# A limit of three loads under way, new orders under that limit, and the first keys issued first, in a fused attention and expert kernel

## The chip, the cores and the metric

The kernel runs on one core of one Trainium2 chip. The metric is device time in microseconds (us): the median of several runs, and beside it one execution taken by the hardware profiler. The engines are named as in the profile: PE is TensorE's matrix multiplication and PEld its weight loads, DVE is VectorE, ACT is ScalarE, POOL is GpSimd, SP is SyncE, which issues most DMA transfers.

## What is computed

Attention over 8 samples, 12 heads, 448 positions and head size 64, all in float32, with scores capped by a tanh; then, per sample, the 128 positions with the highest gate scores go through a two-layer expert.

```python
scores = q @ k^T / sqrt(64)
scores = cap * tanh(scores / cap)                     # cap is 30
attn   = exp(scores - max) / (sum + 1e-9)
x      = (attn @ v), heads side by side               # 8 x 448 x 768
s      = x @ w_gate
top    = the 128 rows of a sample with the largest s
out[top] = x[top] + sigmoid(s[top]) * (relu(x[top] @ w1) @ w2)   # w1 768x1024, w2 1024x768
out[others] = x[others]
```

## The kernel before

The work is cut into 24 "doubles": three groups of four heads for each of the 8 samples. A double needs three loads (`Double.load`, line 620 issues them): queries, keys and values, each of about 450 KB, into rings of two buffers with a third that is lent at the start (`qlent`, `klent`, `vlent`). Its keys are taken in four chunks, three of 128 and one of 64; the two 64-chunks of neighbouring doubles share one unit. For each unit TensorE writes scores into PSUM (`scores_mm`, lines 681 and 691), ScalarE takes the tanh (lines 1252 and 1298) and then the exponential (lines 1261 and 1305) into a buffer `p`, and TensorE multiplies by the values (`values_mm`, line 706), summing over the four chunks in the one PSUM accumulator `psV`. Before the next double may start its values, `evac` (lines 737 to 743) empties that accumulator on VectorE in two halves. From the fifth double on, queries and keys are split into a high and a low part (lines 647 and 653, VectorE), and the scores are three matmuls instead of one.

Six PSUM banks (`psE`) serve the scores at first, so that the scores of one unit are written while ScalarE reads those of another; two of them are needed later for the expert's matmuls. After `SIX` units (20) the six are closed, four become the one score buffer `psS`, and two become `psT`, in which everything of the expert stage is computed.

The weights come in 14 tiles (`weights_proc`, line 555): six of 512 KB and eight of 384 KB, over three staging buffers (`stage` twice, `hs`). VectorE splits each into two parts (lines 567 and 570). The gate weights (`load_gate`, line 541) are one load of 576 KB. When a sample's three doubles are scored (line 772), `select_proc` finds the 128 rows: the scores go to memory and come back as a row (lines 810 and 813), VectorE ranks them (lines 842 and 850) and writes a one-hot matrix (line 881), TensorE picks the row numbers (line 891), and GpSimd gathers the rows (line 909). `expert_proc` transposes them (line 938), multiplies by w1 and w2 in `group` (line 992), and scatters the result (line 1058); the last sample goes through `halves` (lines 1086 and 1104).

The order of all instructions is set when the program is built. `Sim` is a planner: each `Task` has an engine, an estimated duration, what it depends on and which buffers it takes; each engine takes the task that can start first, with ties settled by priorities, which the table `EARLIER` shifts task by task. For TensorE the string `SCRIPT` says which kind comes next: `Q` is the scores of a unit (or half of one), `V` the values of one, and a number behind a letter is how many expert matmuls may come in before. The numbers of the planner put no instruction into the program; they only set its order. On the chip the engines run their instructions in this order and wait for each other by semaphores.

TensorE's instructions have three shapes here: quarter (64 rows by 64 columns: the unsplit scores and the 64-key chunks of the values), tall (128 by 64: the other values) and wide (everything else: split scores and the expert).

The program starts with `first_loads` (lines 1573 to 1578): queries, the cap, the first keys and the rest of the first double, before a branch on the cap's size (line 1714). `warm_up` multiplies zeros on TensorE from line 1588 on until the first keys are there.

Of the kernel before, what the change touches and what calls it, by code (L numbers as in the profile page):

```python
# [8 lines left out]
F32 = mybir.dt.float32  # L9
# [7 lines left out]
P = 128  # L17
# [12 lines left out]
HOLD = 1000  # L30

# [4 lines left out]
SCRIPT = ("Q Q Q1 V Q3 Q V Q4 Q24 V Q1 V2 Q6 Q9 V6 Q1 Q V12 Q Q38 Q V6 Q12 V Q Q15 Q V5 Q3 Q12 "  # L36
# [6 lines left out]

EARLIER = {('evac', 0): -0.4, ('evac', 1): 0.4, ('evac', 3): 0.4, ('evac', 4): -3, ('evac', 5): -1,
           ('evac', 6): 3, ('evac', 7): -3, ('evac', 9): -1, ('evac', 10): 3, ('evac', 11): -3,
           ('evac', 12): 0.4, ('evac', 13): -0.4, ('evac', 17): 1, ('evac', 20): 3, ('evac', 22):
           -1, ('evac', 23): 0.4, ('evac', 25): 3, ('evac', 26): -1, ('evac', 27): 0.4, ('evac',
           28): 0.4, ('evac', 29): 1, ('evac', 30): 1, ('evac', 31): 1, ('evac', 33): 1, ('evac',
           34): -0.4, ('evac', 35): 0.4, ('evac', 36): 1, ('evac', 37): -3, ('evac', 38): 0.4,
           ('evac', 39): 0.4, ('gate', 0): -0.4, ('gate', 1): -3, ('gate', 3): 1, ('gate', 4):  # L50
           -0.4, ('gate', 5): 1, ('gate', 6): 1, ('gate', 7): -0.4, ('gate', 8): 3, ('gate', 11):
           1, ('gate', 12): -1, ('gate', 13): 0.4, ('gate', 14): 3, ('gate', 15): -0.4, ('gate',
# [146 lines left out]

QUARTER, TALL, WIDTH = range(3)  # L200
SWITCH = 40
AFTER = {(TALL, WIDTH): 104, (TALL, QUARTER): 102, (QUARTER, WIDTH): 90, (QUARTER, TALL): 70,
         (WIDTH, TALL): 100, (WIDTH, QUARTER): 60}
MARGIN = 150
RESERVE = 50000
# [1577 lines left out]
```

## Time and profile before

| | us |
|---|---|
| median of 3 runs | 437.09 (436.97 to 438.45) |
| the profiled execution, its own time | 437.59 |
| its span, first to last instruction | 435.8 |
| PE busy in the span | 420.6 |
| ACT busy in the span | 305.7 |
| DVE busy in the span | 278.9 |

The span is what the profiler's trace covers; 1.8 us of the execution's own time lie around it. A busy time is the sum over an engine's instructions, counted once where they overlap. An idle time in a row of the trace stands in square brackets behind the instruction that ended it, with what released it. "issue" there means that nothing the profile shows was waited for. Matmuls are pipelined and their ends are modelled, so a PE busy time holds small pauses too.

### The profile page before, as it was taken

The numbers are of one execution on the slowest core, as the hardware profiler recorded it, in microseconds if no ns is written. First come the engines' busy times: TensorE is split into PE (matmuls) and PEld (weight loads), VectorE is DVE, ScalarE is ACT, GpSimd is POOL, SyncE is SP. The second block draws the span as 40 slices with busy tenths as digits, with TensorE's granted clock in tenths as the row PEclk, the third lists the DMA queues.
The fourth block names the chain that finished last, engine by engine and source line by source line (L and its number), as shares of the span: only waits on it lengthen the run. The fifth ranks groups of instructions, "written<-read, shape, count | busy, mean of one in ns | idle before, by whom it ended". The sixth has DMA issues, their size and how long they took to land.

```text
span 435.8 us, 17858 instructions
## 1 busy us (share of the span) xinstructions
PE 420.6 (96%) x8080; PEld 354.6 (81%) x8080; DVE 278.9 (64%) x862; ACT 305.7 (70%) x197; POOL 26.9 (6%) x73
## 2 busy tenths in 40 slices
PE   8989998999999999999999999999999999999994
PEld 5646677788789888899889978989788898879894
DVE  1586978859852788559754885837937685267241
ACT  5999999697895588695697676969787698411000
POOL 1100010100010000010000100101000010000101
PEclk9999999899999999999999999999999999999998
DMA  7996558370460481373170470463361421230202
GB/s 232 396 388 199 169 161 262 106 240 27 120 259 3 137 267 31 107 245 108 44 282 15 144 245 17 122 214 106 90 236 43 127 86 47 74 69 2 74 3 77
DMA packets 33268, 60.73 MB, mean 139 GB/s; under 512 B 10304, under 2 KB 20288, under 8 KB 33184
## 3 DMA queue, kind: packets, MB, share of 16 engines
q1 hardware_dynamic: 31600, 52.73, 37.4%
q0 software_dynamic: 1440, 6.56, 4.8%
q8 instruction: 65, 1.06, 1.0%
q10 hardware_dynamic: 144, 0.23, 0.1%
q14 instruction: 19, 0.16, 0.1%
HBM read 45.33 MB, written 14.17 MB: 137 GB/s over the span
## 4 chain that ended last, share of the span: by engine, by line
PE 82%; DMA 6%; ACT 5%; DVE 3%; issue 2%; SPq 0%; POOL 0%; POOLq 0%; DVEq 0%; ACTq 0%
PE psV L706 29%; PE psT L992 23%; PE psS L681 16%; PE psB L992 4%; PE psS L691 3%; DMA vlent<-in_v 2%; DMA stage<-in_moe_w 2%; PE psE L681 2%; PE psE L691 2%; ACT p L1252 2%; ACT p L1261 1%; PE psT L938 1%; PE psV L992 1%; DMA p<-out,idx 1%; ACT plent L1261 1%
## 5 line engine op out<-in xcount | busy, mean ns | idle before, releaser
L706 PEld LDWEIGHTS psV<-v,p 128*64 128x64 f32 (+1 forms) x3864 | 104.8, 137 | 21.7 <-issue 15.1
L706 PE MATMUL psV<-v,p 128*64 128x65 f32 (+1 forms) x3864 | 111.6, 223 | 4.5 <-issue 2.4
L1298 ACT ACTIVATE p<-psS,sc 128x1792 f32<-128x1792 f32 x48 | 84.1, 1753 | 39.1 <-PE psS L681 23.2
L1305 ACT ACTIVATE p<-p,capc 128x1792 f32<-128x1792 f32 x48 | 86.1, 1794 | 1.4
L681 PE MATMUL psS<-qh,kh 64*128 64x448 f32 x220 | 43.1, 388 | 0.0
L706 PEld LDWEIGHTS psV<-v,plent 128*64 128x64 f32 (+1 forms) x1288 | 34.7, 137 | 7.9 <-issue 3.0
L737 DVE RECIPROCAL rec<-psV 128x7 f32<-128x7 f32 x48 | 9.5, 199 | 48.5 <-PE psV L706 48.5
L1298 ACT ACTIVATE plent<-psS,sc 128x1792 f32<-128x1792 f32 x16 | 28.0, 1753 | 17.7 <-PE psS L681 8.9
L706 PE MATMUL psV<-v,plent 128*64 128x65 f32 (+1 forms) x1288 | 37.4, 222 | 1.9 <-POOL vlent L667 1.2
L772 DVE CUSTOM_DVE_ANT_0 jk<-xn,gates 128x256 bf16<-128x256 f32 x72 | 30.3, 421 | 1.5
L1305 ACT ACTIVATE plent<-plent,capc 128x1792 f32<-128x1792 f32 x16 | 28.7, 1793 | 0.5
L738 DVE TENSOR_TENSOR xn<-psV,rec 128x384 f32<-128x384 f32 x48 | 26.8, 557 | 1.7
L1261 ACT ACTIVATE p<-p,capc 128x1792 f32<-128x1792 f32 x14 | 25.1, 1792 | 0.5
L1252 ACT ACTIVATE p<-psE,sc 128x1792 f32<-128x1792 f32 x14 | 24.3, 1738 | 0.9 <-PE psE L681 0.5
L842 DVE TENSOR_SCALAR_CACHE_REDUCE jk<-row,score 128x512 bf16<-128x512 f32 (+1 forms) x32 | 23.7, 742 | 0.9
L681 PEld LDWEIGHTS psS<-qh,kh 64*128 64x128 f32 x220 | 20.9, 187 | 2.6 <-ACT p L1298 0.2
L647 DVE CAST kh<-k 128x896 fp32r<-128x896 f32 x20 | 12.5, 626 | 14.0 <-PE psS L681 10.6
L681 PE MATMUL psS<-qlent,kh 64*128 64x448 f32 x112 | 20.9, 370 | 0.0
L681 PE MATMUL psS<-qh,klent 64*128 64x448 f32 x112 | 20.9, 370 | 0.0
L992 PE MATMUL psT<-w2h,hh 64*128 64x384 f32 x192 | 20.3, 340 | 0.6 <-POOL fence L975 0.6
L992 PE MATMUL psT<-w2l,hh 64*128 64x384 f32 x192 | 20.7, 336 | 0.0
L691 PE MATMUL psE<-q,k 64*64 64x448 f32 x176 | 19.7, 548 | 0.4 <-ACT p L1252 0.4
(180 smaller groups left out, 686.4 us busy)
## 6 DMA issues: line engine op xcount, KB each, us to landing
v<-in_v SPq DMA_DIRECT2D x23, 455.0 KB, 4.4
q<-in_q SPq DMA_DIRECT2D x22, 448.0 KB, 5.5
k<-in_k SPq DMA_DIRECT2D x22, 448.0 KB, 6.0
out<-xn SPq DMA_DIRECT2D x24, 384.0 KB, 4.7
stage<-in_moe_w SPq DMA_DIRECT2D x4, 512.0 KB, 8.5
stage<-in_moe_w SPq DMA_DIRECT2D x5, 384.0 KB, 4.4
row<-line SPq DMA_DIRECT2D x7, 256.0 KB, 3.6
out<-xt SPq DMA_DIRECT2D x48, 32.0 KB, 4.0
```

The lines of the kernel that those rows point to most:

```text
L647: nc.vector.tensor_copy(t.slots[0].obj, self.at(nm))
L681: done += [tc.nc.tensor.matmul(banks[2 * r + j][:, :K.S], lhsT=a[HALF[j], r, c * P:(c + 1) * P], rhs=b[HALF[j], r, :], start=(n == 0), sto ...
L691: done += [tc.nc.tensor.matmul(banks[n][HALF[half], :K.S], lhsT=k[HALF[j], r, at:at + HD], rhs=q[HALF[j], r, :], start=True, stop=True).ins]
L706: tc.nc.tensor.matmul(D.acc.obj[HALF[g], r, i * WIDE:(i + 1) * WIDE], lhsT=p[rows, h, n * HD:(n + 1) * HD], rhs=v[rows, u, :], start=(c == ...
L738: nc.vector.tensor_tensor(slots[0].obj.rearrange("p c (r j d) -> p r j c d", r=2, j=2)[:, r], blocks[:, :2 * full, :K.D].rearrange("p (j c ...
L772: nc.vector.tensor_tensor_reduce(out=K.jk[:, :x.shape[1]], in0=x, in1=g, scale=1.0, scalar=0.0, op0=ALU.mult, op1=ALU.add, accum_out=part[ ...
L842: nc.vector.tensor_scalar(K.jk[:m], row[:m], score[:m, c:c + 1], None, op0=ALU.is_gt, op1=ALU.add, accum_out=rk.obj[:m, 0, c:c + 1])
L992: ins = nc.tensor.matmul(bank.obj[:, g, :width], lhsT=pair.obj[part][HALF[h], i, :], rhs=K.wts[r][HALF[h], i, g * width:(g + 1) * width], ...
L1252: a = nc.scalar.activation(slot.obj, K.S6[:, 2 * lo:2 * lo + 4, :K.S], AF.Tanh, scale=K.sc)
L1261: nc.scalar.activation(slot.obj, slot.obj, AF.Exp, scale=K.cap)
L1298: nc.scalar.activation(slot.obj, K.S4[:, :, :K.S], AF.Tanh, scale=K.sc)
L1305: nc.scalar.activation(slot.obj, slot.obj, AF.Exp, scale=K.cap)
```

## The change

Four things are done.

1. At most three loads are under way. `in_flight` keeps the loads of the doubles, of the weights and of the gate weights in one list, and each from the fourth on waits on SP, by a semaphore, for the landing of the one three places before. The planner knows this limit too (`Sim.ready`). Stores and the row DMAs are not counted.
2. The planner has other costs: one price per shape that TensorE changes into (`AFTER`), durations of matmul groups, and a price for the fetching of TensorE's own instructions in blocks of 256 (`stall`). `SIX` is 19 instead of 20. `SCRIPT` and `EARLIER` are new. A scatter also waits in the plan for the one before it (`SWEEP`).
3. The first keys are the first DMA on SP; the cap goes to ACT's queue, behind the first queries.
4. `warm_up` multiplies a constant tile of zeros instead of one that VectorE first clears.

```diff
 HOLD = 1000
+SWEEP = 400
+CHUNK, FIRST_EDGE, BEGUN, FETCH, SHARE, DEEP = 256, 193, 71, 2350, 0.5, 8000
+LOADS = 3
+LOAD = ("load", "wload", "wg")
...
-SCRIPT = ("Q Q Q1 V Q3 Q V Q4 Q24 V Q1 V2 Q6 Q9 V6 Q1 Q V12 Q Q38 Q V6 Q12 V Q Q15 Q V5 Q3 Q12 "
+SCRIPT = ("Q3 Q Q12 V29 Q20 Q18 V26 Q2 Q V16 Q2 V4 Q16 Q8 Q14 V1 Q6 V Q6 Q14 V Q20 Q V2 Q2 Q Q "
...
-EARLIER = {('evac', 0): -0.4, ('evac', 1): 0.4, ('evac', 3): 0.4, ('evac', 4): -3, ('evac', 5): -1,
+EARLIER = {('evac', 0): -0.4, ('evac', 1): 1, ('evac', 5): 3, ('evac', 6): 0.4, ('evac', 7): -0.4,
...
-AFTER = {(TALL, WIDTH): 104, (TALL, QUARTER): 102, (QUARTER, WIDTH): 90, (QUARTER, TALL): 70,
-         (WIDTH, TALL): 100, (WIDTH, QUARTER): 60}
+AFTER = (141, 141, 195)
...
-SIX = 20
+SIX = 19
...
+            busy += self.stall(start, busy, task.size)
...
+            if task.kind in LOAD:
+                self.loads.append(task)
...
+    def stall(self, start, busy, n):
+        add, count = 0, self.count
+        while n and self.edge <= count + n:
+            at = start + busy * ((self.edge - count) / n) + add
+            if self.fetched > at:
+                add += self.fetched - at
+                at = self.fetched
+            self.fetched = at + FETCH + SHARE * min(max(self.dma - at, 0), DEEP)
+            self.edge += CHUNK
+        self.count = count + n
+        return add
+
+    def ready(self, task):
+        r = task.ready()
+        if r is not None and task.kind in LOAD and len(self.loads) >= LOADS:
+            r = max(r, self.loads[-LOADS].t)
+        return r
...
+def in_flight(tc, K, ins):
+    if K.loose:
+        return
+    K.flight.append(ins)
+    if len(K.flight) > LOADS:
+        tc.add_manual_dep(ins, K.flight[-LOADS - 1].name,
+                          mybir.DependencyInfo(mybir.DependencyClass.Sync,
+                                               mybir.DependencyReason.DATA),
+                          reason="loads in flight")
...
-    tc.nc.sync.dma_start(K.gates, K.w_gate)
+    in_flight(tc, K, tc.nc.sync.dma_start(K.gates, K.w_gate).ins)
...
-            nc.sync.dma_start(t.tile[:, :m], w[i * P:(i + 1) * P, :])
+            in_flight(tc, K, nc.sync.dma_start(t.tile[:, :m], w[i * P:(i + 1) * P, :]).ins)
...
-            tc.nc.sync.dma_start(s.obj, src[self.d])
+            in_flight(tc, K, tc.nc.sync.dma_start(s.obj, src[self.d]).ins)
...
-    yield Task("POOL", 1300, scatter, deps=[end], reads=[xe, idx], lag=2400, prio=1,
-               kind="scatter")
+    yield Task("POOL", 1300, scatter, deps=[end, (K.swept, SWEEP)], reads=[xe, idx], lag=1700,
+               prio=1, kind="scatter")
...
     nc.scalar.dma_start(q[:, 0], K.qd[D.d][:, 0])
-    nc.sync.dma_start(K.cap, cap.to_broadcast([P, 1]))
     nc.sync.dma_start(k[:, :, :2 * HD], K.kd[D.d][:, :, :2 * HD])
+    nc.scalar.dma_start(K.cap, cap.to_broadcast([P, 1]))
...
-    zero = K.xe.slots[0].obj[:, :P]
-    nc.vector.memset(zero, 0.0)
+    zero = nc.const_aps.tensor(0.0, [P, P], F32)
```

How the change moves instructions is shown at three places. A row is a line of the source, the operation, out<-in and the shape, and how many follow each other (x2).

The first is SP's queue behind the branch at the start; `_88`, `_90` and `_92` are the second double's queries, keys and values, `klent`, `qlent` and `vlent` those of the third. Before:

```order
L620 DMA q_88<-in_q 128x896
L555 DMA stage<-in_moe_w 128x1024
L620 DMA k_90<-in_k 128x896
L555 DMA hs<-in_moe_w 128x1024
L555 DMA stage<-in_moe_w 128x1024
L620 DMA v_92<-in_v 128x910
L541 DMA gates<-in_moe_w_gate 128x1152
L555 DMA stage<-in_moe_w 128x1024
L620 DMA klent<-in_k 128x896
L620 DMA k_89<-in_k 128x896
L620 DMA vlent<-in_v 128x910
L620 DMA qlent<-in_q 128x896
```

After the change:

```order
L586 DMA stage<-in_moe_w 128x1024 x2
L651 DMA q_88<-in_q 128x896
L651 DMA k_90<-in_k 128x896
L586 DMA hs<-in_moe_w 128x1024
L586 DMA stage<-in_moe_w 128x1024
L651 DMA v_92<-in_v 128x910
L586 DMA stage<-in_moe_w 128x1024
L651 DMA klent<-in_k 128x896
L651 DMA k_89<-in_k 128x896
L586 DMA hs<-in_moe_w 128x1024
L586 DMA stage<-in_moe_w 128x768 x2
L651 DMA qlent<-in_q 128x896
```

Two weight tiles now come before the second double's queries and keys, its keys are the fourth load and so wait for the first tile to land, the third double's queries have become the fourteenth load (they were the eleventh), and the gate weights and `vlent` come later than these rows.

The second is where the six score banks are closed, on TensorE and on VectorE; `psE` is the six banks, `psS` the four, `v_92` the fifth double's values and `v_91` the sixth's. TensorE before:

```order
L706 MATMUL psV<-v_92,p_93 64x65 x28
L706 MATMUL psV<-v_92,p_94 64x65 x28
L681 MATMUL psE<-qh_107,kh_105 128x448 x2
L681 MATMUL psE<-qlent,kh_105 128x448 x2
L681 MATMUL psE<-qh_107,klent 128x448 x2
L681 MATMUL psE<-qh_107,kh_105 128x448 x2
L681 MATMUL psE<-qlent,kh_105 128x448 x2
L681 MATMUL psE<-qh_107,klent 128x448 x2
L706 MATMUL psV<-v_91,p_94 64x65 x28
L681 MATMUL psS<-qh_107,kh_105 128x448 x2
L681 MATMUL psS<-qlent,kh_105 128x448 x2
L681 MATMUL psS<-qh_107,klent 128x448 x2
```

TensorE after the change:

```order
L737 MATMUL psV<-v_92,p_93 64x65 x28
L737 MATMUL psV<-v_92,p_94 64x65 x28
L712 MATMUL psS<-qh_107,kh_105 128x448 x2
L712 MATMUL psS<-qlent,kh_105 128x448 x2
L712 MATMUL psS<-qh_107,klent 128x448 x2
L712 MATMUL psS<-qh_107,kh_105 128x448 x2
L712 MATMUL psS<-qlent,kh_105 128x448 x2
L712 MATMUL psS<-qh_107,klent 128x448 x2
L922 LDWEIGHTS sel_117
L922 MATMUL psT<-vals_71,sel_117 128x5
```

The unit that was the last in `psE` is now the first in `psS`; behind it come the pick of the first sample's rows (eight matmuls from `sel_117`), a second unit in `psS`, and only then the sixth double's first values (`v_91,p_94`), which before stood between the two units. VectorE there, from the end of the ranking on, before:

```order
L865 TENSOR_TENSOR vals_71<-rk_120,vals_71 128x4
L737 RECIPROCAL rec_103<-psV 128x7
L738 TENSOR_TENSOR xn_97<-psV,rec_103 128x2x3x64
L743 TENSOR_SCALAR xt_100<-psV,rec_103 128x64
L881 TENSOR_SCALAR sel_117<-iota,rk_120 128x128 x4
L772 ISA jk,part_80<-xn_97,gates 128x256
```

VectorE after the change:

```order
L678 CAST kh_104<-k_90 128x896
L912 TENSOR_SCALAR sel_117<-iota,rk_120 128x128 x4
L768 RECIPROCAL rec_102<-psV 128x7
L769 TENSOR_TENSOR xn_98<-psV,rec_102 128x2x3x64
L774 TENSOR_SCALAR xt_99<-psV,rec_102 128x64
L684 TENSOR_TENSOR kl_108<-k_90,kh_104 128x896
L931 COPY both_77<-psT 128x5
L932 TENSOR_TENSOR both_77<-both_77,psT 128x5
L933 SCALAR_TENSOR_TENSOR idx_124<-both_77 128x1
L935 TENSOR_TENSOR gt_127<-both_77 128x1
L936 TENSOR_TENSOR gt_127<-gt_127,both_77 128x1
L768 RECIPROCAL rec_103<-psV 128x7
```

Before, the accumulator's second half was emptied (`rec_103`) ahead of the one-hot matrix; now the one-hot matrix is first, and a split (`kl_108`) and the reading of the pick stand between the two halves.

The third is TensorE at the end of the twelfth double, an example of how the later order differs; before:

```order
L706 MATMUL psV<-v_91,plent 64x65 x28
L706 MATMUL psV<-v_91,p_93 64x65 x28
L706 MATMUL psV<-v_91,p_94 64x65 x28
L691 MATMUL psS<-q_87,k_90 64x448 x4
L691 MATMUL psS<-q_88,k_89 64x448 x4
L706 MATMUL psV<-v_91,p_95 64x65 x28
L992 MATMUL psT<-w1l,xh 128x512 x8
L992 MATMUL psT<-w1h,xl 128x512 x12
```

After the change:

```order
L737 MATMUL psV<-v_91,plent 64x65 x28
L737 MATMUL psV<-v_91,p_93 64x65 x28
L737 MATMUL psV<-v_91,p_94 64x65 x28
L737 MATMUL psV<-v_91,p_95 64x65 x28
L722 MATMUL psS<-q_88,k_90 64x448 x4
L722 MATMUL psS<-q_87,k_89 64x448 x4
L1023 MATMUL psT<-w1h,xh 128x512 x12
L1023 MATMUL psT<-w1l,xh 128x512 x6
```

The double's four groups of values now stand together, and the scores that stood between them follow, so that TensorE changes shape less often here. Counted over the whole fast path in the order of TensorE's matmuls, it changes into tall 46 times before and 43 after, into wide 43 and 37, into quarter 36 and 36: 125 and 116 in all. Behind the last values of the last double the order of TensorE's instructions is the same as before, but for four matmuls that stand on the other side of a transpose.

## Rows read from the trace of the kernel before

**Rows 1.** Busy time by stretch: stretch, length, each engine's busy us (instructions), granted PE clock, DMA share, GB/s.

```profile
10.40:24.00 13.60, 12.25 (x280) 7.58 (x280) 8.83 (x16) 13.47 (x8) 1.76 (x8) 1.00 1.01 398
24.00:33.00 9.00, 8.14 (x168) 4.63 (x170) 7.37 (x16) 8.14 (x6) 0.20 (x2) 1.00 1.04 383
52.00:77.00 25.00, 22.49 (x541) 18.14 (x545) 20.75 (x71) 23.60 (x15) 1.45 (x3) 1.00 0.69 212
77.00:81.00 4.00, 4.00 (x86) 3.35 (x77) 2.46 (x11) 2.21 (x2) 0.12 (x1) 0.59 0.41 121
81.00:200.00 119.00, 117.78 (x2426) 102.84 (x2424) 81.92 (x252) 92.73 (x59) 7.06 (x16) 1.00 0.45 142
200.00:379.50 179.50, 179.01 (x3643) 157.20 (x3638) 115.55 (x378) 136.78 (x86) 9.21 (x24) 1.00 0.38 118
379.50:435.80 56.30, 49.85 (x511) 44.15 (x500) 26.19 (x86) 4.62 (x9) 5.18 (x9) 0.97 0.15 44
```

**Rows 2.** Timeline of the start: start us, duration us, engine, line, operation [idle before <-releaser].

```profile
0.83 0.39 SPq L1574 DMA_DIRECT2D capc<-in_cap  x1
0.83 0.40 ACTq L1573 DMA_DIRECT2D q<-in_q  x1
1.27 0.71 SPq L1575 DMA_DIRECT2D k<-in_k  x1
4.85 1.56 PE L691 MATMUL psV<-q,k 64*64 64x448 f32 x8
5.30 0.34 SPq L620 DMA_DIRECT2D q<-in_q  x1
6.54 1.01 ACT L1156 ACTIVATE p<-psV,sc 128x896 f32<-128x896 f32 x1 [2.00 <-PE psV L691]
```

**Rows 3.** Timeline around the pause at 30 us, PE, PEld and ACT.

```profile
28.78 1.72 PE L691 MATMUL psE<-qlent,klent 64*64 64x448 f32 x11
30.84 0.20 PEld L691 LDWEIGHTS psE<-qlent,klent 64*64 64x64 f32 x7 [1.11 <-issue]
31.86 1.76 ACT L1252 ACTIVATE plent<-psE,sc 128x1792 f32<-128x1792 f32 x1 [0.80 <-PE psE L691]
```

**Rows 4.** DMA queues from 28 to 29 us: packets, MB, share of 16 engines.

```profile
q1 hardware_dynamic: 260, 0.32, 97.7%
q8 instruction: 1, 0.02, 5.9%
```

**Rows 5.** DMA issues in small windows: count, KB, us from issue to landing.

```profile
v<-in_v SPq DMA_DIRECT2D x1, 455.0 KB, 3.5
...
q<-in_q SPq DMA_DIRECT2D x1, 448.0 KB, 6.3
...
qlent<-in_q SPq DMA_DIRECT2D x1, 448.0 KB, 8.1
```

**Rows 6.** Timeline where the six banks are closed, VectorE, PE and ACT.

```profile
71.15 1.73 ACT L1252 ACTIVATE p<-psE,sc 128x1792 f32<-128x1792 f32 x1
76.34 0.28 DVE L743 TENSOR_SCALAR xt<-psV,rec 128x64 f32<-128x64 f32 x1
76.72 1.05 PE L706 MATMUL psV<-v,p 64*64 64x65 f32 x56 [1.80 <-issue]
78.97 0.58 PE L681 MATMUL psS<-qh,kh 64*128 64x448 f32 x2
```

**Rows 7.** Pieces of the chain that ended last: start us, us, what.

```profile
80.41 3.78 PE psV L706 x112
...
88.15 1.42 PE psS L681 x12
...
91.90 1.22 PE psS L681 x12
...
98.76 3.42 PE psV L706 x112
...
117.12 1.78 PE psV L706 x56
```

More of the change, by code (lines that the diff above doesn't have):

```diff
@@ L332, in finish @@
             if task.shape != self.shape:
-                busy += AFTER.get((self.shape, task.shape), 0)
+                busy += AFTER[task.shape] if self.shape is not None else 0
             self.shape = task.shape
+            busy += self.stall(start, busy, task.size)
         end = start + busy
@@ L378, in candidate @@
                 pick = task
-        return max(best, pick.ready()), pick
+        return max(best, self.ready(pick)), pick
     def run(self):
@@ L999, in mm @@
                     tc.add_manual_dep(ins, gap[0].name, order, reason="rows change banks")
-        t = Task("PE", cost, mm, deps=[parts[i][part]] + (passed if m == last + 1 else []), take=[] if m else [K.banks],
+        t = Task("PE", cost, mm, size=4, deps=[parts[i][part]] + (passed if m == last + 1 else []), take=[] if m else [K.banks],
                  refs=[] if m else [2], reads=[pair] if m == 2 * last + 1 else [], prio=prio,
@@ L1025, in expert_proc @@
         yield [p for pair in parts.values() for p in pair]
-    bank, t = yield from group(tc, K, "w1", (1, 0 if K.tail else b), xs, parts, "w1", K.ND, K.F // 2, 231)
+    bank, t = yield from group(tc, K, "w1", (1, 0 if K.tail else b), xs, parts, "w1", K.ND, K.F // 2, 232)
     relus = []
@@ L1087, in mm @@
                                  rhs=K.wts[r][:, i, cols], start=(m == 0), stop=(m == last))
-            t = Task("PE", 173, mm, deps=[parts[i][part]], take=[] if m else [K.banks],
+            t = Task("PE", 173, mm, size=2, deps=[parts[i][part]], take=[] if m else [K.banks],
                      refs=[] if m else [1], reads=[hp] if g and m == last else [], prio=(1, b),
@@ L1238, in emit @@
             self.u, self.half = self.u + self.half, 1 - self.half
-        task = Task("PE", 780 if shape == QUARTER else 615, emit, shape=shape, reads=reads,
-                    kind="scores")
+        task = Task("PE", 750 if shape == QUARTER else 606, emit, shape=shape, reads=reads,
+                    kind="scores", size=16 if shape == QUARTER else 12)
         task.seq = 0
@@ L1288, in emit @@
             self.S_free = None
-        task = Task("PE", 1560 if shape == QUARTER else 1230, emit, shape=shape, reads=reads,
-                    kind="scores")
+        task = Task("PE", 1500 if shape == QUARTER else 1212, emit, shape=shape, reads=reads,
+                    kind="scores", size=32 if shape == QUARTER else 24)
         task.seq = 0
@@ L1353, in emit @@
                 D.values.t = t.t
-        task = Task("PE", 1680 if shape == TALL else 870, emit, shape=shape,
-                    reads=[D.pslot[c], D.v.slots[0]], kind="values")
+        task = Task("PE", 1630 if shape == TALL else 815, emit, shape=shape,
+                    reads=[D.pslot[c], D.v.slots[0]], kind="values", size=112)
         task.seq = 0
```

294 lines of the change are left out of this document (147 added, 147 removed), and 44 rows, old and new, of tables (EARLIER, SCRIPT).

## The prediction

> **What bounds the kernel now.** I read the busy time by stretch first, since the whole span hides that the kernel has three parts [rows 1]. Up to 77 us ScalarE is the bound: in the stretches 10.4 to 24, 24 to 33 and 52 to 77 it is busy 13.47 of 13.60 us, 8.14 of 9.00 and 23.60 of 25.00. Scores are written, ScalarE takes tanh and exponential, and TensorE has almost nothing else to do yet. From 81 to 379.5 us TensorE is the bound: busy 117.78 of 119.00 us and 179.01 of 179.50, so 1.7 us of idle time in 298.5. From 379.5 us on the last sample's selection and expert run as a chain; TensorE is busy 49.85 of 56.30 us there. Between the first two parts lie 4 us, 77 to 81, at a granted clock of 0.59 [rows 1].
>
> So a gain must come from ScalarE's delays before 77 us, from the passage between the parts, from less TensorE work after 81 us, or from the tail. All idle time of TensorE in the six stretches up to 379.5 us is 1.35 + 0.86 + 2.51 + 0 + 1.22 + 0.49 = 6.4 us; no transfer bounds a long stretch, though the DMA engines are full (share 1.0) from 10.4 to 33 us.
>
> Then the timeline. At the start, TensorE's first scores begin at 4.85 us and ScalarE's first tanh, waiting for them, at 6.54 [rows 2]. Around 30 us TensorE's weight loads stop for 1.11 us with no releaser, inside a run of scores, and ScalarE sits idle for 0.80 us behind them [rows 3]; in the microsecond from 28 to 29 the data queue took 97.7% of the 16 DMA engines, and one packet of the instruction queue took 5.9%, which is 0.94 us of one engine [rows 4]. I read this as TensorE waiting for its own code behind data. At 76.72 us TensorE starts the sixth double's values after 1.80 us of idle time; the releaser is given as "issue", but VectorE's last step of emptying the accumulator ends at 76.34 + 0.28 = 76.62 [rows 6], so I read it as that. Right after this idle time the clock is at its lower level (0.59 over 4 us), and a split-score matmul takes 0.58 us.
>
> **The change, part by part.** The sum is made against the profiled execution's own 437.59 us, 0.5 above the median of 437.09.
>
> *First keys first.* SP issues them at 0.83 instead of 1.27 us, 0.44 sooner. The cap moves behind ACT's first DMA (0.40 us) [rows 2], so the flag on which all engines branch comes about 0.4 later. ScalarE's first tanh waits for the scores, not for the flag, so most of the gain should arrive: **-0.3 us**, ends -0.44 and +0.4. The zero tile of the warm-up is taken as 0: the warm-up only fills the wait for the keys, and it starts no later than now.
>
> *Three loads under way.* It adds no instruction on the engines that compute, only waits on SP. Behind a waiting load on SP stand stores and the row DMAs; the stores free buffers that are taken two doubles later, so they have many us. What it can take away is the pause at 30 us. Where that was, loads took 8.1 us to land, against 3.5 with little else under way [rows 5]. With fewer data packets ahead, the block of instructions comes sooner. ScalarE's 0.80 us is on the path there [rows 3]; I take 0.6 of it and 0.2 for smaller pauses: **-0.8 us**, ends 0 and -1.2.
>
> *SIX = 19 and the order there.* The nineteenth unit's tanh begins at 71.15 and ends at 72.88 [rows 6]; less the two terms above, 71.8. Then the first unit in the four banks can start at 71.9 and takes 1.4 us behind values [rows 7], the pick follows, the second unit can start when the next tanh (1.73) is done, near 75.1, and takes 1.2, so the sixth double's chunk (1.05 [rows 6]) starts near 76.4 and the tall values behind it near 77.4. Before, these started at 80.41 [rows 7], behind the late chunk, twelve slow matmuls and the pick. So 3.0 us at best, of which 1.1 are counted above: 1.9. Against it stands VectorE: the one-hot matrix, a split and the reading of the pick now precede the accumulator's second half, so the chunk may still wait; and if TensorE idles long, the clock falls again. The bad end is that the wait of 1.80 stays as it is and half of the tanh between the two units is not covered, 0.9. I take **-1.0 us**, between ends -1.9 and +0.9, nearer the good one because the values no longer stand between the two units.
>
> *Fewer changes of shape.* The same scores take 1.42 us behind values and 1.22 behind wide work, so entering wide costs 0.20; one group of values takes 1.78 us, two in a row 3.42, so entering tall costs 2 x 1.78 - 3.42 = 0.14 [rows 7]. Six and three fewer: 6 x 0.20 + 3 x 0.14 = **-1.6 us**. TensorE is 99% busy where they fall, so nothing hides this; it could be paid back as waits (below). Ends -1.6 and 0.
>
> *The rest of the new order.* The 1.7 us of idle time after 81 us may go or come elsewhere: **0**, ends -1.7 and +3. GpSimd's scatters, gathers and fences move by a few places in its queue; it is busy 7.06 of 119 us there [rows 1], so that is 0 too. The tail has the same order on TensorE and no loads: **0**, ends ±0.5. Planner costs that emit nothing: 0.
>
> Sum: -0.3 - 0.8 - 1.0 - 1.6 = -3.7, so 433.9 for a profiled execution, and **433.4 us** for the median.
>
> A rule that speaks against the second term: the Trainium skill (Runtime: NRT & Kernel Launch, Instruction fetch mechanics) says an engine fetches its next block while it runs the present one, so that crossing a block is mostly hidden; and DMA: Bandwidth & Descriptors (Queues, rings and completion order) says that a DMA engine takes its queues in turn, packet by packet, so that a queue of data would not hold a fetch for long. The pause of 1.11 us at a full data queue speaks against "hidden" here, but no run here shows the turn-taking. By these pages the second term would be 0 and the median 434.2.
>
> **The rivals.** *The limit frees nothing.* The pause at 30 us is not set by how many loads wait: three loads of 450 KB still fill the DMA engines. For it: the DMA share would stay near 1.0 in that stretch, since the same bytes must come. Against it: landing times of 8.1 against 3.5 us. The second term is 0: 434.2.
>
> *The new order opens waits where it closed others.* An order fitted to planned times has TensorE stand wherever a time is off. For it: the idle time after 81 us was already only 1.7 us, so a new order can hardly better it; and VectorE empties the accumulator late at the six banks' end. Price: third term +0.9 instead of -1.0, and twice the idle time after 81 us: 433.4 + 1.9 + 1.7 = 437.0, no change.
>
> *The limit starves the start.* Loads now go in threes, each waiting for one to land, and weight tiles are ahead. The third double's queries are the fourteenth load. SP starts near 5.7 us (the branch row at 5.30 plus 0.4 for the cap); with a landing time L, the fourteenth lands at about 5.7 + 5L. They were used at 28.78 [rows 3], so they are due near 28.5, and L may be 4.6 us. A value load with little beside it took 3.5 us, a query load among a few took 6.3 [rows 5]. At the stretch's rate of 398 GB/s [rows 1] three loads of 455 KB (1.4 MB) take 3.5 us. At L = 5.5 they land at 33.2, 4.7 late, on ScalarE's path: 438.1. At 6.3: 37.2, 8.7 late, 442.1. Slower than before from L = 5.3 on. Against it: with three under way no load waits behind six others, so I expect 3.5 to 4.6.
>
> **How the numbers follow.** Forecast 0.58, the limit frees nothing 0.12, new waits 0.17, starved start 0.13. The range: at the low end the better ends of the terms (-0.44 - 1.2 - 1.9 - 1.6 - 1.7 = -6.8, so 430.3 for the median) and 0.8 us for pauses inside TensorE's busy time that I can't see, 429.5; at the high end the new waits with a little more, 437.5. That leaves out most of the starved start and the edges, under 0.2. A measurement of this kernel can tell about 0.5%, 2.2 us, so faster means below 434.9 and slower above 439.3. Faster: 0.55 of the forecast's 0.58 and 0.07 of the first rival, 0.62. Slower: 0.08 of the starved start and 0.02 of the new waits, 0.10. The rest, 0.28, is the same.
>
> **What would show it.** Right: the first tanh 0.1 to 0.4 us earlier than 6.54; no gap on ScalarE near 30 us; no load landing later than 5 us; the first scores in four banks near 72 us and no stretch at a clock near 0.59; about 116 changes of shape and idle time after 80 us of about 2 us; a tail of some 56 us from the last values on. Wrong: ScalarE waiting for scores of `qlent` or of the second double's keys before 40 us (starved); a TensorE wait for `evac` or a clock dip near 75 us as large as before (third term); idle time of TensorE over 4 us between 80 and 375 us (new waits); the pause still there with the landing times short (the limit frees nothing).

## The result, and the profile after

The changed kernel took 439.56 us (median of 12 runs, 435.79 to 442.32) against 437.49 for the kernel before (12 runs, 435.88 to 438.91): a ratio of 1.0056, 95% interval 1.0032 to 1.0080. It is slower by 0.56%. I had forecast 433.4 us, faster; the prediction was wrong in sign. The profiled execution took 439.84 us with a span of 438.1, so 2.25 us more than the one of before (437.59).

Busy time by stretch of the changed kernel (columns as in [rows 1]):

```profile
10.40:24.00 13.60, 12.62 (x281) 7.50 (x277) 10.57 (x15) 13.47 (x9) 1.13 (x4) 1.00 0.90 297
24.00:33.00 9.00, 6.57 (x180) 4.60 (x182) 5.49 (x10) 7.79 (x5) 0.00 (x0) 1.00 0.91 304
33.00:52.00 19.00, 15.56 (x279) 9.78 (x276) 14.28 (x35) 13.86 (x9) 0.25 (x2) 0.91 0.86 288
52.00:77.00 25.00, 24.65 (x623) 19.26 (x621) 16.86 (x51) 24.61 (x15) 1.98 (x4) 1.00 0.55 165
77.00:81.00 4.00, 2.81 (x50) 2.03 (x44) 3.83 (x18) 3.57 (x3) 0.00 (x0) 0.96 0.65 215
81.00:200.00 119.00, 118.85 (x2410) 103.14 (x2410) 83.91 (x265) 92.73 (x58) 7.42 (x17) 0.99 0.45 144
200.00:379.50 179.50, 179.36 (x3638) 157.69 (x3636) 117.83 (x384) 136.66 (x85) 9.12 (x24) 1.00 0.38 119
```

Two things stand out beside [rows 1]. Data comes at 297 and 304 GB/s where it came at 398 and 383. And from 33 to 52 us, where ScalarE was busy 18.80 of 19.00 us before, it is busy only 13.86, and the granted clock falls to 0.91 on the mean. The row of the kernel before:

```profile
33.00:52.00 19.00, 18.61 (x417) 11.74 (x412) 14.96 (x33) 18.80 (x12) 0.39 (x1) 1.00 0.55 173
```

After 81 us, on the other hand, TensorE is idle for 0.15 + 0.14 = 0.29 us, against 1.22 + 0.49 = 1.71 before.

The timeline of the changed kernel says what happened (ScalarE, VectorE, PE, PEld, and SP's issues):

```profile
6.16 1.01 ACT L1193 ACTIVATE p<-psV,sc 128x896 f32<-128x896 f32 x1 [1.01 <-PE psV L722]
...
30.01 0.21 PEld L722 LDWEIGHTS psE<-qlent,klent 64*64 64x64 f32 x8 [1.55 <-DMA qlent<-in_q]
31.82 1.75 ACT L1289 ACTIVATE plent<-psE,sc 128x1792 f32<-128x1792 f32 x1 [1.14 <-PE psE L722]
...
36.00 0.33 SPq L586 DMA_DIRECT2D hs<-in_moe_w  x1
...
41.39 0.56 DVE L598 CAST w2h<-hs 128x768 fp32r<-128x768 f32 x1 [2.09 <-DMA hs<-in_moe_w]
41.87 0.20 DVE L768 RECIPROCAL rec<-psV 128x7 f32<-128x7 f32 x1
...
42.57 0.28 DVE L774 TENSOR_SCALAR xt<-psV,rec 128x64 f32<-128x64 f32 x1
...
42.95 3.16 PE L737 MATMUL psV<-vlent,plent 128*64 128x65 f32 x56 [3.44 <-issue]
...
47.33 1.75 ACT L1289 ACTIVATE p<-psE,sc 128x1792 f32<-128x1792 f32 x1 [5.01 <-PE psE L722]
```

The first tanh starts 0.38 us earlier than before (6.16 against 6.54 [rows 2]). At 30 us the pause in TensorE's code is gone [rows 3], but in its place TensorE waits for the third double's queries, and ScalarE loses 1.14 us instead of 0.80. The large loss is the next one. A weight tile (`hs`) is issued at 36.00 and is there only at 41.39. VectorE waits for it 2.09 us. Behind that cast on VectorE stands the second half of emptying the second double's accumulator (41.87 to 42.85), and TensorE may not start the third double's values before that is done: 42.95. TensorE works off its order too, so the scores behind these values come late, and ScalarE stands idle for 5.01 us. None of this has anything to do with the tile's own use: TensorE's first matmul with this weight matrix (`w2h`) starts at 124.49 us.

The idle time also cost clock. In the stretches behind it and behind the passage:

```profile
42.90:46.10 3.20, 3.15 (x60) 3.06 (x60) 2.83 (x5) 0.00 (x0) 0.00 (x0) 0.54 0.89 249
...
80.60:83.30 2.70, 2.65 (x16) 1.91 (x17) 2.56 (x10) 1.01 (x3) 1.02 (x2) 0.52 0.03 11
```

The 56 values at 42.95 took 3.16 us; the same group takes 1.85 at the full clock. At the passage the first unit in `psS` starts at 77.32 without waiting, but the second waits until the tanh of the first has read `psS`, and runs at the low clock, and the sixth double's values follow at 83.26:

```profile
77.32 0.47 PE L712 MATMUL psS<-qh,kh 64*128 64x448 f32 x2
...
80.66 0.74 PE L712 MATMUL psS<-qh,kh 64*128 64x448 f32 x2 [0.79 <-ACT plent L1335]
...
83.26 3.20 PE L737 MATMUL psV<-v,p 64*64 64x65 f32 x112
```

The start of ScalarE's tanhs is a good ruler, since they come in the same order in all these kernels (us, from the timelines; each column is one execution, so a few tenths mean little):

| tanh no. | before | changed | `no_limit` | `split_behind` | `before_limit` | `evac_ahead` |
|---|---|---|---|---|---|---|
| 8 | 27.50 | 27.11 | 27.14 | 27.20 | 27.71 | 26.91 |
| 9 | 31.86 | 31.82 | 30.60 | 30.67 | 31.17 | 30.95 |
| 12 | 42.27 | 47.33 | 42.14 | 41.65 | 46.56 | 43.77 |
| 20 | 71.15 | 75.34 | 70.14 | 69.69 | 75.08 | 73.35 |
| 22 | 80.33 | 84.08 | 78.84 | 77.45 | 82.44 | 80.36 |

So the changed kernel is 0.4 us ahead at the eighth tanh, level at the ninth, 5.1 behind at the twelfth, 4.2 at the twentieth, 3.8 at the twenty-second, and 2.2 at the last values (the expert matmuls behind them start at 381.76 against 379.56). From there both take the same: 438.1 - 381.76 = 56.3 us and 435.8 - 379.56 = 56.2.

### The profile page after: what moved, and what is told of

The parts are those of the page before. It is cut to its first block, busy times and chain, and to the rows that moved or that the text cites. A ratio compares the mean times of both kernels' runs of the same rounds, so it can differ in the third digit from the quotient of the medians.

```text
span 438.1 us, 17847 instructions
## 1 busy us (share of the span) xinstructions
PE 421.1 (96%) x8080; PEld 355.6 (81%) x8080; DVE 280.9 (64%) x865; ACT 302.9 (69%) x193; POOL 27.6 (6%) x73
## 4 chain that ended last, share of the span: by engine, by line
PE 81%; DMA 8%; ACT 7%; issue 2%; DVE 1%; POOL 0%; SPq 0%; ACTq 0%; POOLq 0%; DVEq 0%
PE psV L737 29%; PE psT L1023 23%; PE psS L712 17%; PE psB L1023 4%; PE psS L722 3%; ACT p L1289 2%; DMA stage<-in_moe_w 2%; DMA hs<-in_moe_w 2%; ACT p L1298 2%; PE psE L722 2%; PE psT L969 1%; DMA qlent<-in_q 1%; DMA p<-out,idx 1%; PE psV L1023 1%; ACT plent L1298 1%
## 5 line engine op out<-in xcount | busy, mean ns | idle before, releaser
L712 PE MATMUL psS<-qh,kh 64*128 64x448 f32 x224 | 44.4, 393 | 0.8 <-ACT plent L1335 0.8
L1335 ACT ACTIVATE plent<-psS,sc 128x1792 f32<-128x1792 f32 x17 | 29.7, 1748 | 11.4 <-PE psS L712 6.9
L1342 ACT ACTIVATE plent<-plent,capc 128x1792 f32<-128x1792 f32 x17 | 30.5, 1791 | 0.5
L1023 PE MATMUL psT<-w1l,xh 64*128 64x512 f32 x144 | 20.2, 392 | 0.0
```

The lines of the kernel that those rows point to most:

```text
L712: done += [tc.nc.tensor.matmul(banks[2 * r + j][:, :K.S], lhsT=a[HALF[j], r, c * P:(c + 1) * P], rhs=b[HALF[j], r, :], start=(n == 0), sto ...
L1023: ins = nc.tensor.matmul(bank.obj[:, g, :width], lhsT=pair.obj[part][HALF[h], i, :], rhs=K.wts[r][HALF[h], i, g * width:(g + 1) * width], ...
L1335: nc.scalar.activation(slot.obj, K.S4[:, :, :K.S], AF.Tanh, scale=K.sc)
L1342: nc.scalar.activation(slot.obj, slot.obj, AF.Exp, scale=K.cap)
```

## The experiments

Theory A: the limit is the loss. With three loads under way data comes more slowly, a load that nobody needs soon comes late, and VectorE, which works in order, waits for it with urgent work behind. Theory B: the new order is the loss, with weight tiles ahead of what ScalarE needs. The ratios are to the kernel before, run beside it on the same chip; the median of the kernel before differs by up to 2 us between chips, so medians from different chips are not compared.

**The limit away, the order kept** (`no_limit`), and **five loads** (`limit_five`: 5 for 99). `LOADS` stays 3 for the planner, so every engine's order is that of the changed kernel.

```diff
-LOADS = 3
+LOADS, UNDER_WAY = 3, 99
...
-    if len(K.flight) > LOADS:
-        tc.add_manual_dep(ins, K.flight[-LOADS - 1].name,
+    if len(K.flight) > UNDER_WAY:
+        tc.add_manual_dep(ins, K.flight[-UNDER_WAY - 1].name,
```

> The changed kernel with the same order on every engine, but no load waits for the landing of an earlier one. Theory A, the limit is the loss: with three loads under way only some 300 GB/s arrive between 10 and 33 us, the weight tile that VectorE needs near 39.3 us lands at 41.39, the emptying of the accumulator stands behind it, and ScalarE waits 5.0 us. Then without the limit the tile is there, ScalarE's wait of 5.0 near 42 us is under 1 us, and the time falls by about 5 us from the changed kernel's 439.6, to 434 to 435.5. Theory B, the new order is the loss: the weight tiles now stand ahead of what ScalarE waits for, whatever the limit; then the wait near 42 us stays over 3 us and the time stays at 438.5 to 440.5. The pause of PE's weight loads near 30 us (1.11 us before) may come back: 0 to 0.8 us of ScalarE.

> The changed kernel with the same order on every engine and five loads under way instead of three. Theory A (the limit is the loss): most of the rate of 398 GB/s of the kernel before is back, ScalarE's wait near 42 us is under 2 us, 434.5 to 437. Theory B (the order is the loss): as the changed kernel, 438.5 to 440.5.

Measured: `no_limit` 0.9970 (0.9942 to 0.9998), `limit_five` 0.9996 (0.9970 to 1.0021). Timeline of `no_limit`:

```profile
30.60 1.74 ACT L1289 ACTIVATE plent<-psE,sc 128x1792 f32<-128x1792 f32 x1
...
37.75 0.56 DVE L598 CAST w2h<-hs 128x768 fp32r<-128x768 f32 x1 [0.36 <-DMA hs<-in_moe_w]
...
38.94 0.27 DVE L774 TENSOR_SCALAR xt<-psV,rec 128x64 f32<-128x64 f32 x1
...
39.31 1.85 PE L737 MATMUL psV<-vlent,plent 128*64 128x65 f32 x56 [1.50 <-issue]
...
42.14 1.75 ACT L1289 ACTIVATE p<-psE,sc 128x1792 f32<-128x1792 f32 x1 [1.05 <-PE psE L722]
```

The tile is there at 37.75 instead of 41.39, the values start at 39.31 at the full clock, and ScalarE's 5.01 us are 1.05. The order is the same, so theory B is out: the difference between 1.0056 and 0.9970, 0.86% or 3.8 us, is the limit's. Theory A had expected about 5 us and a wait of ScalarE under 1 us here; it was 1.05. With five under way ScalarE's wait is 1.48 us, under 2 as expected, but of the 398 GB/s only 313 came back. At 30 us ScalarE waits for nothing, with no limit at all.

**The limit alone, in the old order** (`before_limit`): `in_flight` and its three calls from the change, nothing else.

> The kernel before with its own order, and the limit of three loads alone added. Theory A (the limit is the loss wherever it stands): loads bring about 300 GB/s from 10 us on instead of 398, the third double's queries (the eleventh load) land near 5.3 + 4 x 5.2 = 26 us, so they are in time, but the weight tiles behind them come later and VectorE waits for them; 439 to 443, slower than before's 437.5. Theory B (the new order is the loss, the limit is harmless): 436.5 to 437.9. My prediction's second term: no pause of PE's weight loads near 30 us, ScalarE's 0.80 us there gone, 436.7.

Measured: 1.0160 (1.0124 to 1.0196), 7.0 us slower, more than the 5.5 us at the upper end of theory A. Its timeline:

```profile
29.08 0.21 PEld L703 LDWEIGHTS psE<-qlent,klent 64*64 64x64 f32 x8 [0.16 <-DMA qlent<-in_q]
...
38.04 0.56 DVE L579 CAST w2h<-stage 128x768 fp32r<-128x768 f32 x1 [1.74 <-DMA stage<-in_moe_w]
...
39.51 0.20 DVE L749 RECIPROCAL rec<-psV 128x7 f32<-128x7 f32 x1
...
41.11 0.27 DVE L755 TENSOR_SCALAR xt<-psV,rec 128x64 f32<-128x64 f32 x1
...
41.49 3.30 PE L718 MATMUL psV<-vlent,plent 128*64 128x65 f32 x56 [3.03 <-issue]
...
46.56 1.75 ACT L1264 ACTIVATE p<-psE,sc 128x1792 f32<-128x1792 f32 x1 [4.90 <-PE psE L703]
```

The same chain in another order, around other tiles: VectorE waits for weights (4.26 us for one at 31.62, then 0.76 and 1.74), the accumulator is emptied late, the values run at the low clock, ScalarE loses 4.90 us. The third double's queries, expected at 26 us, are there at 29.08, and ScalarE loses nothing by it (its ninth tanh starts at 31.17). In this order they are the twelfth load, not the eleventh, as the sections before the result count. So the limit costs 7.0 us in the old order and 3.8 in the new: an order found with the limit pays a little over half as much for it.

**The first keys alone** (`keys_first`): the third and fourth part of the change in the kernel before.

```diff
-    nc.sync.dma_start(K.cap, cap.to_broadcast([P, 1]))
     nc.sync.dma_start(k[:, :, :2 * HD], K.kd[D.d][:, :, :2 * HD])
+    nc.scalar.dma_start(K.cap, cap.to_broadcast([P, 1]))
...
-    zero = K.xe.slots[0].obj[:, :P]
-    nc.vector.memset(zero, 0.0)
+    zero = nc.const_aps.tensor(0.0, [P, P], F32)
```

> The kernel before with the third and fourth part of the change alone: the first keys are the first DMA on SP, the cap goes to ACT's queue, the warm-up multiplies a constant tile; the orders stay. If the first 0.38 us that the changed kernel's first tanh is earlier (6.16 instead of 6.54) reach the end: 437.0 to 437.2, 0.3 to 0.5 below before. If they are lost in a later wait for a load: 437.5. The flag comes later, and SP's first load behind the branch at 5.9 instead of 5.3; if that delays a load that is waited for: 438.

Measured: 0.9987 (0.9965 to 1.0008), 0.6 us faster on the mean, not told apart from nothing. Its trace gave more than its time. From 24 to 33 us:

```profile
24.00:33.00 9.00, 8.70 (x212) 6.12 (x212) 8.02 (x17) 8.90 (x6) 0.64 (x1) 1.00 0.98 347
```

ScalarE is busy 8.90 of 9.00 us here, with the loads of the kernel before in their old order, no limit, and the DMA engines 98% busy. The pause at 30 us, for whose removal I had credited the limit with 0.8 us, is not there in this execution, without any limit. The low clock at the passage, 0.59 in [rows 1], is absent too, though TensorE waits 1.39 us there and the order is the old one:

```profile
70.00:85.00 15.00, 13.59 (x386) 11.35 (x384) 13.74 (x46) 12.74 (x10) 1.20 (x2) 1.00 0.58 177
...
75.43 1.05 PE L706 MATMUL psV<-v,p 64*64 64x65 f32 x56 [1.39 <-issue]
```

So neither the pause nor the low clock comes with this order in every execution, and one profile of a kernel can't tell what a change did to either.

**How the rate depends on the number under way** (`limit_two`: 2 for 99 in the first diff).

> The changed kernel with two loads under way instead of three, the same order. Theory A (the limit is the loss, because what is under way bounds the rate): with three some 300 GB/s came from 10 to 33 us; with two it should be about two thirds of it, 200 to 230, each load landing in 3.5 to 4.5 us; everything of the first 80 us comes later, and the time rises by more than 10 us over the changed kernel, ratio over 1.03. If the rate is not bounded by the number under way (two already fill the engines): 290 to 300 GB/s as with three, ratio 1.005 to 1.012.

Measured: 1.0235 (1.0194 to 1.0277). From 10.4 to 33 us:

| kernel | loads under way | GB/s | DMA share | ScalarE busy of 22.6 us | ratio |
|---|---|---|---|---|---|
| `limit_two` | 2 | 230 | 0.72 | 18.61 | 1.0235 |
| changed | 3 | 300 | 0.91 | 21.26 | 1.0056 |
| `limit_five` | 5 | 313 | 0.91 | 22.37 | 0.9996 |
| `no_limit` | no limit | 327 | 0.94 | 22.37 | 0.9970 |
| before | no limit, old order | 392 | 1.02 | 21.60 | 1 |

The rate with two is 230, three quarters of that with three, and the time rises, though by less than the 3% I had expected. Beyond three the rates are hard to tell apart: in the four kernels here with three under way, which differ in their order, they are 288 (`before_limit`), 300, 311 (`evac_ahead`) and 315 (`both_limit`). From 10.4 to 24 us the rate still grows with the number (223, 297, 333 and 345 GB/s with two, three, five and no limit), from 24 to 33 us it doesn't (240, 304, 284 and 300). The clock drops with two as well:

```profile
24.00:33.00 9.00, 5.27 (x102) 3.90 (x104) 6.01 (x11) 5.14 (x4) 0.00 (x0) 0.63 0.74 240
```

**Which loads matter** (`weights_free`): only the doubles' loads count and wait.

```diff
-    in_flight(tc, K, tc.nc.sync.dma_start(K.gates, K.w_gate).ins)
+    tc.nc.sync.dma_start(K.gates, K.w_gate)
...
-            in_flight(tc, K, nc.sync.dma_start(t.tile[:, :m], w[i * P:(i + 1) * P, :]).ins)
+            nc.sync.dma_start(t.tile[:, :m], w[i * P:(i + 1) * P, :])
```

> The changed kernel, where only the doubles' loads (queries, keys, values) count in the limit of three and wait; weight tiles and gate weights are issued as their buffers come free, in the same place of SP's queue. Theory A1 (the late weight tile with the emptying behind it is most of the loss): the tile lands before 39 us and ScalarE's wait near 42 us is under 1.5 us; ratio 0.996 to 1.000. Theory A2 (the doubles' own loads are late too, and a load that waits on SP holds up the weight tile behind it): 1.001 to 1.006.

Measured: 0.9937 (0.9903 to 0.9971). All of the limit's cost is gone, and 335 GB/s come from 10.4 to 33 us. The signs of theory A1 came, and the ratio is better than the 0.996 it had at best:

```profile
37.01 0.56 DVE L598 CAST w2h<-hs 128x768 fp32r<-128x768 f32 x1 [0.56 <-DMA hs<-in_moe_w]
...
41.40 1.75 ACT L1289 ACTIVATE p<-psE,sc 128x1792 f32<-128x1792 f32 x1 [0.68 <-PE psE L722]
...
76.92 4.11 PE L737 MATMUL psV<-v,p 64*64 64x65 f32 x112 [0.72 <-issue]
```

So what costs is counting the weights. That a limit on queries, keys and values would be harmless is a weaker reading: up to 45 us SP issues each of these loads right behind the issue ahead of it here, so what is left of the limit hardly ever waits. The kernel is not told apart from `no_limit` (0.9970), whose interval overlaps.

**The weight tile behind the emptying** (`evac_ahead`): the limit stays; on VectorE one cast comes after the emptying instead of before it. Here and in the next three kernels line numbers are 9 higher.

```diff
+BEHIND = {('whi', 9): ('evac', 3)}
...
-        task.fn(task)
+        if getattr(task, 'name', None) in BEHIND:
+            self.held[BEHIND[task.name]] = task
+        else:
+            task.fn(task)
+        t = self.held.pop(getattr(task, 'name', None), None)
+        if t:
+            t.fn(t)
```

> The changed kernel with its limit of three loads and one thing moved on VectorE: the first step on the weight tile that landed at 41.39 us comes behind the emptying of the second double's accumulator (second half) instead of ahead of it. Theory A1, the late tile costs because VectorE waits for it in order with the emptying behind it: the emptying ends near 40.3 instead of 42.85, the third double's values start near 40.3 instead of 42.95 and at the full clock, ScalarE's wait of 5.0 us near 42 falls to 1 to 2.5, and the time falls by 2.5 to 4 us: 0.994 to 0.999 of before (the changed kernel: 1.0056). Theory A2, all loads are late and ScalarE would meet the next late one: the wait moves to the next tile, the fourth double's queries or the gate weights; less than 1 us gained, 1.003 to 1.006.

Measured: 1.0004 (0.9972 to 1.0035), 2.3 us better than the changed kernel (the two intervals just touch) and between the ranges of the two theories, 0.994 to 0.999 and 1.003 to 1.006. Its timeline shows why it is not more:

```profile
39.19 0.28 DVE L783 TENSOR_SCALAR xt<-psV,rec 128x64 f32<-128x64 f32 x1
...
40.02 0.98 PE L731 MATMUL psE<-q,k 64*64 64x448 f32 x8 [2.25 <-DMA q<-in_q]
...
40.96 0.56 DVE L607 CAST w2h<-hs 128x768 fp32r<-128x768 f32 x1 [1.50 <-DMA hs<-in_moe_w]
...
43.77 1.75 ACT L1298 ACTIVATE p<-psE,sc 128x1792 f32<-128x1792 f32 x1 [2.31 <-PE psE L731]
```

The accumulator is now empty at 39.47, before the tile lands at 40.96. But TensorE meets the next late load, the fourth double's queries, waits 2.25 us for them, and ScalarE still loses 2.31. The sixteenth tanh, at 59.47, loses 1.73 us by the same chain one emptying later: that one ends only at 55.69, behind weight steps for which VectorE waited 1.50, 1.02 and 0.68 us and gate weights for which it waited 0.88. So by the means somewhat over half of the limit's cost (2.3 of 3.8 us) is VectorE's wait for weights ahead of this one emptying; that the rest is other late loads is read from this one profile.

**The split behind the emptying, without the limit** (`split_behind`), then **both moves** with the limit (`both_limit`) and without (`both_free`). The second entry for the table above moves a part of a split of keys (`kl`) at the passage:

```diff
-BEHIND = {('whi', 9): ('evac', 3)}
+BEHIND = {('low', 4): ('evac', 9)}
```

> The changed kernel without the limit (ratio 0.997), and one thing moved on VectorE at the passage: the low part of a split of keys (1.08 us) comes behind the emptying of the accumulator's second half instead of ahead of it and of the reading of the pick. Theory C, this split is why my third term did not come: the sixth double's values start near 77.0 instead of 78.01, right behind the second unit's scores; if the clock then stays up, these 112 matmuls take 3.4 instead of 5.03 us and the scores behind them 1.7 instead of 2.29: together 2 to 3.2 us less, ratio 0.990 to 0.9925. If the clock falls all the same: 1 us less, 0.9945. Rival D, the passage is bound by ScalarE (the second unit waits for the tanh of the first): less than 0.5 us gained, 0.996 to 0.997.

> The changed kernel with its limit and both moves on VectorE. If the limit costs by the two waits of VectorE alone (A1 and C): as without the limit and with both moves, 0.988 to 0.992. If the limit costs by late loads as such (A2): 1.000 to 1.004.

> The changed kernel without the limit and with both moves. Without the limit the emptying ended at 39.2 behind the tile that landed at 37.75 and the third double's values waited 2.25 us; with the emptying first they start near 38.3, about 0.9 us earlier, and ScalarE's 1.1 us wait for them goes. If C holds: 0.988 to 0.992, the fastest of all. If neither move matters without the limit: 0.997.

Measured: `split_behind` 0.9917 (0.9886 to 0.9949), `both_limit` 1.0003 (0.9977 to 1.0030), `both_free` 0.9912 (0.9878 to 0.9947). VectorE and TensorE at the passage in `no_limit`:

```profile
75.20 1.08 DVE L684 TENSOR_TENSOR kl<-k,kh 128x896 fp32r<-128x896 f32 x1
...
76.93 0.20 DVE L768 RECIPROCAL rec<-psV 128x7 f32<-128x7 f32 x1
...
77.64 0.28 DVE L774 TENSOR_SCALAR xt<-psV,rec 128x64 f32<-128x64 f32 x1
...
78.01 5.03 PE L737 MATMUL psV<-v,p 64*64 64x65 f32 x112 [1.07 <-issue]
```

and in `split_behind`:

```profile
75.55 0.20 DVE L777 RECIPROCAL rec<-psV 128x7 f32<-128x7 f32 x1
...
76.25 0.28 DVE L783 TENSOR_SCALAR xt<-psV,rec 128x64 f32<-128x64 f32 x1
76.44 1.08 DVE L693 TENSOR_TENSOR kl<-k,kh 128x896 fp32r<-128x896 f32 x1
76.63 4.10 PE L746 MATMUL psV<-v,p 64*64 64x65 f32 x112
```

One VectorE instruction of 1.08 us stood ahead of the emptying and of the reading of the pick. With it behind, the values start 1.38 us earlier and without a wait. Of that, 0.45 us were there before the passage (twentieth tanh 69.69 against 70.14). From the second unit (75.46 and 74.98) to the values it is 2.55 us against 1.65, so the move itself gives 0.9. The values also take 4.10 instead of 5.03 us, since the clock is low for less of them, but in `weights_free`, with the split still ahead, they take 4.11, so that is not shown to be the move's. From 0.9970 to 0.9917 is 0.53%, 2.3 us by the means for one move; the two intervals just touch, the two kernels ran on different chips, each against the kernel before there, and only the 0.9 us is seen in the rows. So the ratio is theory C's (0.990 to 0.9925), but not its clock: that fell, and for this 0.9945 had been expected, which the interval still holds.

With the limit both moves together (1.0003) are no better than `evac_ahead` (1.0004); what theory A1 with C had expected, 0.988 to 0.992, did not come; the 1.000 to 1.004 that I had expected if late loads cost as such did. The timelines give a reason. Under the limit the split has nothing to hold up: in `evac_ahead`, where it is still ahead, the emptying ends at 79.11 and the values start right behind their scores, whose unit had waited 1.75 us for ScalarE's tanh:

```profile
78.84 0.27 DVE L783 TENSOR_SCALAR xt<-psV,rec 128x64 f32<-128x64 f32 x1
...
80.11 4.36 PE L746 MATMUL psV<-v,p 64*64 64x65 f32 x112
```

And in `both_limit` late loads cost elsewhere. In its profiled execution (434.30, one of its fastest runs) the fourth double's queries are in time, but the third double's are 2.32 us late, ScalarE loses 1.79 at the ninth tanh, and at the sixteenth an emptying that comes late, behind a weight tile for which VectorE waited 2.35 us at 43.15, holds up TensorE and then ScalarE again:

```profile
54.15 0.28 DVE L783 TENSOR_SCALAR xt<-psV,rec 128x64 f32<-128x64 f32 x1
...
54.52 1.05 PE L746 MATMUL psV<-v,p 64*64 64x65 f32 x56 [1.41 <-issue]
...
58.19 1.75 ACT L1298 ACTIVATE p<-psE,sc 128x1792 f32<-128x1792 f32 x1 [1.62 <-PE psE L721]
```

Moving one cast takes away one place where a late load is met, not the lateness.

`both_free` and `split_behind` beat both kernels: the one before by 0.9% and 0.8%, the changed one by more. But what was expected of the weight cast's move without the limit did not come: in `both_free` the third double's values start at 39.15 and not near 38.3, ScalarE still waits 1.07 us, and 0.9912 against 0.9917 is no gain.

## Why the prediction was wrong, step by step

*First keys first, -0.3.* Right in kind: -0.38 us at the first tanh, -0.39 still at the eighth. That it hit the size is in part luck: the first tanh starts between 5.59 and 6.44 us in the ten profiles with the new start, and at 6.54 and 6.75 in the two with the old one. The changed kernel then lost it in a wait for a load; alone it measured 0.6 us, with an interval that holds 0.

*Three loads under way, -0.8, between 0 and -1.2.* This step failed, and with it the sign. It measured +3.8 us in the new order and +7.0 in the old. Three things in it were wrong.

First, I named what stands behind a waiting load on SP (stores, row DMAs) and stopped there. The wait on SP makes the load late, and the engine that uses the load then waits with its own queue behind it. That engine was VectorE, on a weight tile with plenty of time to spare, and its queue held the emptying on which TensorE and then ScalarE depend.

Second, the gain. I read the pause at 30 us as TensorE's code waiting behind data and let the limit remove it. It is absent in `keys_first` and in `no_limit`, with the data queue nearly as full. What it hangs on is open; the limit is not needed to be rid of it. The page on queues that I had cited against this step (DMA: Bandwidth & Descriptors, Queues, rings and completion order, of the Trainium skill) would have put the gain at 0, and the limit did gain nothing here; but no run shows the turn-taking, and the pause of the one profile of the kernel before stays unexplained.

Third, the landing time. I took 3.5 to 4.6 us, from 1.4 MB at 398 GB/s and a lone load of 3.5 [rows 5]. The third double's queries, the fourteenth load of the new order, were there at 30.0 us; with my own formula, 5.7 + 5L, L was 4.9. The rate of 398 was that of a full queue; under the limit it was 300. The Trainium skill (DMA: Bandwidth & Descriptors, Anatomy of one DMA) puts a fixed 2.0 us beside the time for the bytes, most of it waiting until the last write is confirmed, measured on GpSimd's way of issuing. An estimate from it, 2.0 us and the time of N loads of 0.47 MB at the 398 GB/s of [rows 1], gives 215 GB/s for two under way and 254 for three; measured were 230 and 300, so it is somewhat too dark, but on the right side, and by it L is 5.5, beyond the 5.3 from which I had said the change would be slower.

My third rival, *the limit starves the start*, held in kind, with 0.13. Its place was only the smaller part: the third double's queries came 1.2 us later than used before, and cost 1.14 us in place of the pause of 0.80. It priced ScalarE's direct loads and not the weight tile.

*SIX = 19 and the order there, -1.0.* It did not come in the changed kernel. Read in `no_limit`, whose load waits don't disturb it: I had put the first unit at 71.9, the second at 75.1, the sixth double's values at 76.4; they came at 72.13, 75.46 and 78.01. The scores were right, the values late. I had named the cause as the bad end, that a split and the reading of the pick stand ahead of the emptying, and then taken a value near the good end; `split_behind` shows that the split takes 0.9 us there, and 2.3 by the means. The clock I had put under an "if" (if TensorE idles long), and the sum went without it. TensorE did idle before the second unit, and with that came a low clock in several kernels: 0.64 from 76.6 to 80.6 in `split_behind`, 0.53 from 76.9 to 83 in `no_limit`. Not in all: in `both_limit` TensorE waits 1.63 us before the second unit, the clock stays 1.00, and the values take 2.83 us:

```profile
72.00:83.00 11.00, 9.37 (x256) 7.38 (x252) 10.48 (x42) 10.57 (x8) 1.50 (x2) 1.00 0.62 192
...
78.81 2.83 PE L746 MATMUL psV<-v,p 64*64 64x65 f32 x112
```

What decides it is open, and so is how much of this term is luck of an execution. (The 0.58 us that the prediction reads as one slow split-score matmul is a row of two.)

*Fewer changes of shape, -1.6.* It fits a count, but is not shown. I priced each order's matmuls and changes as the prediction does and compared with the time that passed from 90 us to the last values: TensorE took 5.4 us more than that sum before, 5.2 in the changed kernel and 4.7 in `no_limit`. Of the 1.6 us some 1.2 lie in that stretch: TensorE changes 33 times into wide tiles and 29 times into tall ones there before, 29 and 26 times after. But its idle time after 81 us fell too, from 1.71 to 0.29 us, and the count can't tell fewer changes from less waiting. No run has the one without the other, and the price of a single change stays untested.

*The rest of the new order, 0.* That fall of the idle time by 1.4 us is a gain which this term did not hold; it and the count above are two readings of the same time, not to be added.

*The tail, 0.* Right: 56.3 against 56.2 us.

Together: +5.1 at the twelfth tanh, of which ScalarE makes good 0.9 by the twentieth, where it had idle time before that is now covered by the delay (23.60 of 25.00 us busy from 52 to 77 us before, 24.61 now); 0.4 at the passage; and some 1.6 behind it, which the shapes or the smaller idle time may account for. That leaves 2.2, against 2.25 measured. Without the limit the forecast's other terms give -2.9 us (-0.66%); `no_limit` measured -0.30% with the passage spoiled, `split_behind` -0.83% with the split moved, and `weights_free` -0.63% with the split in place. That these lie around the forecast is in part luck, since the clock at the passage is not the same in every execution.

## What to carry to other kernels

A limit on transfers under way is a delay for every transfer that it counts. Before adding one, follow each delayed load to the engine that takes it, and read what stands behind that wait on that engine: a load with much slack is dangerous if an in-order engine waits for it with urgent work behind. Leave loads of that kind out of the limit, or move their first use behind the urgent work (here the first gave back all that the limit had cost, the second 2.3 of 3.8 us); and take the rate under the limit from a stretch with as few loads under way, not from a full queue.

## What was not expected of the hardware

- Two loads of about 0.45 MB under way brought 230 GB/s from 10.4 to 33 us, three 288 to 315 in four kernels; five brought 313 and no limit 327 in the same order, but 392 in the order before. So beyond three the order of the loads made more difference than their number; what bounds the rate there is not shown.
- From 38.5 to 42.9 us the changed kernel's TensorE was busy 1.01 of 4.40 us; from 42.9 to 46.1 its granted clock was 0.54, about its lower level (1.2 of 2.4 GHz). I had seen this at the passage only, not as a price of a late load: it is paid for in idle time, and again in the slower work behind it. It doesn't follow each wait: behind one of 1.39 us in `keys_first` and one of 1.63 us in `both_limit`, both at the passage, the granted clock stayed 1.00.
